# Rows of the second x chunk behind the first load, shorter dummy run, full-array last products and a new order in an attention and gated-MLP kernel

## Chip, cores and metric

The kernel runs on one core of a Trainium2 chip. Its metric is the device time of one execution in microseconds (us), as a median over runs. The core has five engines that work side by side, each with its own queue of instructions: TensorE (PE: matmuls, with weight loads shown apart as PEld), VectorE (DVE), ScalarE (ACT), GpSimd (POOL) and SyncE (SP, which here only issues transfers).

## The reference

The two blocks read the same x and are mixed by a gate for each row. S = 2048 rows, D = 512, 32 heads of 16 columns, F = 1376; inputs and output are bf16.

```python
q, k, v = split_heads(x @ wqkv)                       # 32 heads, 16 columns each
p = softmax(einsum("bhqd,bhkd->bhqk", q, k) * 16 ** -0.5)
a = merge_heads(einsum("bhqk,bhkd->bhqd", p, v)) @ wo
b = ((x @ w_gate) * (x @ w_up)) @ w_down
g = sigmoid((x * gate_w).sum(-1, keepdims=True))
out = g * a + (1 - g) * b
```

## The kernel before

**Tiling.** Four chunks of 512 query rows, four blocks of eight heads in each, and each block in two halves of four heads make 32 groups. A group has 16 steps, one for each tile of 128 keys. A step has four cells: a cell is a 128x512 tile of scores in one of the eight PSUM banks (`ps`). Nearly all matmuls use a 64x32 piece of the PE array (`pe64`, lines 1720 to 1730; `held`, line 1704, is the same product on weights that are still in the array). Four such products side by side make one job, and the two halves `r` of the array's rows work as two queues.

**Two ways through the exponential.** A step of kind "A" is exponentiated by ScalarE (`exp`, line 1816), which takes one cell (128x512) or two at once if their banks are neighbours (128x1024). A step of kind "D" goes to VectorE (`dpass`, line 1854), which makes an approximate exponential by integer arithmetic; three shifted copies of it are made by GpSimd or VectorE (`copy`, line 1866), and PE multiplies all four with scaled copies of V (`pv`, line 1748; `Vs`). So a D step costs 24 more matmuls than an A step and no ScalarE time.

**Order of the work.** Nothing loops on the chip. A planner (`_Sched`) runs when the program is built: it keeps a clock of its own, has costs for every job, and at each moment lets each engine take the next job. Its choices are governed by some 40 tables in `PAR`, each a list of runs (count, value), one entry for each microsecond of the planner's clock, read by `g()`. `apair` lets a new pair of score jobs take two banks together (0: no; 1 and 2: two neighbours; 3 and 4: any two if no neighbours are free; with 2 and 4 the job waits when there are none). `dl` is the most D steps in a group; `alook`, `amax`, `dlook` and the like are limits on what is under way. Other scalars tell the planner when things of the head are there: `t0` the first scores, `tx` the chunks of x, `tw` the weights, `sp0` SP's queue. Each engine then executes its list in that order, with semaphore waits.

**The head** (`prologue`, line 2049) is written out by hand. SP and ScalarE's queue each issue two loads of the first 512 rows of x (into a `DB` buffer), then the first 128 columns of wk (SP) and wq (ScalarE's queue). SP goes on with the rows of chunk 1 into `OT` (two loads of 256 KB), eight transposing loads for chunks 2 and 3, the rest of wk and wq, and later the loads into `QM`. GpSimd's queue loads wv and the gate's weights once wk and wq are there. PE runs six dummy products on constants (`dummy`), transposes the first rows, runs five more dummies (`dummy2`, line 2143), and computes the first Q and K (line 2139), from which the first scores follow. Chunk 1 is transposed on PE (`x_turn`, line 1804).

**The tail.** After the last group, `tail_norm` (line 1971) normalises the output of the last half block in two halves of 256 rows, into `OT[:, 3]`. `tail_out` (line 1982) then adds the last product with wo (`wq[:, 1]` holds its rows) to four banks, one for each tile of 128 output rows, scales by the gate, adds the MLP part (`part_`) and stores. Each tile gets its product in two jobs of half the array's rows, which follow one another. Tiles 0 and 2 are finished by one fused VectorE operation; tiles 1 and 3 are scaled by ScalarE into `oc` and `oraw`, and added by GpSimd (tile 1) and VectorE (tile 3).

## Time and profile before

| | |
|---|---|
| median of 3 runs | 660.68 us (659.93 to 662.45) |
| profiled execution | 659.11 us, its span 657.3 us |
| PE busy | 650.2 us (99%), 22739 matmuls |
| ScalarE busy | 640.3 us (97%) |
| VectorE busy | 606.6 us (92%) |
| GpSimd busy | 523.1 us (80%) |
| first scores start | 8.82 us |
| normalisation of the last half block starts | 649.45 us |

The span runs from the first to the last instruction. A row of the profile gives an engine, a line of the kernel, the operation, what it writes and reads with shapes, and a count; behind the bar stand busy time, mean ns of one, and the idle time before with what ended it. PE's busy time counts any matmul under way, and matmuls overlap, so a busy PE may still have room. In rows in order of time the first column is the start, the second the duration.

### The profile page before, as it was taken

How to read it: one execution, taken by the hardware profiler on the slowest of the kernel's cores; microseconds unless marked ns; L12 is line 12 of the kernel's file. 1: busy time of each engine (PE TensorE's matmuls, PEld its weight loads, DVE VectorE, ACT ScalarE, POOL GpSimd, SP SyncE). 2: the span in 40 equal slices, each digit the busy share in tenths (PEclk: the TensorE clock that was granted, in tenths of full speed). 3: DMA queues.
4: the chain of work that ended last, by engine and by line, in shares of the span. 5: the costliest groups of instructions: out<-in, count | busy, mean ns of one | idle time of the engine just before them, and what ended most of it. 6: DMA issues, size and time to landing. Idle time of an engine off the chain costs nothing.

```text
span 657.3 us, 46640 instructions
## 1 busy us (share of the span) xinstructions
PE 650.2 (99%) x22739; PEld 364.1 (55%) x20515; DVE 606.6 (92%) x1002; ACT 640.3 (97%) x812; POOL 523.1 (80%) x607
## 2 busy tenths in 40 slices
PE   8999999999999999999999999999999999999997
PEld 4565555555555654555555655555555665555653
DVE  6999999999998899999999899999999789989895
ACT  5999999999999999999999999999999999999995
POOL 2537898898987978899998889989898859556772
PEclk9999999999999999999999999999999999999999
DMA  9101212221210110101011010100101010000101
GB/s 181 62 4 45 64 42 72 33 57 48 69 46 20 25 34 19 30 6 34 9 23 29 22 44 12 30 13 14 29 6 41 15 47 20 15 22 19 32 9 46
DMA packets 32114, 22.89 MB, mean 35 GB/s; under 512 B 17356, under 2 KB 28524, under 8 KB 31920
## 3 DMA queue, kind: packets, MB, share of 16 engines
q1 hardware_dynamic: 30784, 18.86, 11.5%
q8 instruction: 169, 2.77, 1.7%
q0 software_dynamic: 176, 0.53, 0.3%
q10 hardware_dynamic: 960, 0.52, 0.3%
q14 instruction: 25, 0.20, 0.1%
HBM read 12.23 MB, written 2.36 MB: 22 GB/s over the span
## 4 chain that ended last, share of the span: by engine, by line
PE 98%; DMA 1%; DVE 0%; issue 0%; ACT 0%; ACTq 0%
PE ps L1727 87%; PE ps L1705 10%; DMA wq<-in_A_wqkv_dram 1%; PE ps L2139 0%; DVE hT L2009 0%; DVE hT L2006 0%; ACT wu L1824 0%; ACTq L2056 0%; PE ps L1811 0%; ACTq L82 0%
## 5 line engine op out<-in xcount | busy, mean ns | idle before, releaser
L1727 PE MATMUL ps<-QM,KT 64*32 64x512 bf16 x5968 | 450.4, 378 | 0.3 <-ACT wu L1824 0.3
L1864 DVE TENSOR_SCALAR DB<-ps 128x512 int16<-128x512 f32 x563 | 367.8, 687 | 27.0 <-PE ps L1727 24.0
L1871 POOL INT64_ADD DB<-DB x374 | 330.8, 900 | 75.6 <-DVE DB L1864 19.2
L1824 ACT ACTIVATE PT<-ps 128x1024 bf16<-128x1024 f32 (+1 forms) x368 | 313.5, 950 | 0.5 <-PE ps L1705 0.3
L1727 PE MATMUL ps<-DB,Vs 64*17 64x512 bf16 x3424 | 300.6, 376 | 0.1
L1824 ACT ACTIVATE xT<-ps 128x1024 bf16<-128x1024 f32 (+1 forms) x271 | 240.8, 965 | 0.2
L1727 PEld LDWEIGHTS ps<-QM,KT 64*32 64x32 bf16 x5968 | 135.4, 89 | 146.2 <-DVE DB L1864 34.8
L1705 PE MATMUL ps<-QM,KT 64*32 64x512 bf16 x2224 | 215.9, 376 | 0.0
L1727 PE MATMUL ps<-PT,Vp 64*17 64x512 bf16 x1274 | 176.7, 376 | 0.0
L1727 PE MATMUL ps<-xT,Vp 64*17 64x512 bf16 x974 | 144.8, 376 | 0.0
L1727 PE MATMUL ps<-DB,Vp 64*17 64x512 bf16 x1128 | 109.5, 377 | 0.0
L1727 PE MATMUL ps<-xT,wg 64*32 64x512 bf16 x1376 | 105.8, 376 | 0.0
L1727 PE MATMUL ps<-xT,wu 64*32 64x512 bf16 x1376 | 105.0, 377 | 0.0
L1727 PEld LDWEIGHTS ps<-DB,Vs 64*17 64x17 bf16 x3424 | 81.6, 86 | 30.1 <-PE ps L1727 7.7
L1727 PE MATMUL ps<-wd,hT 64*32 64x512 bf16 x1408 | 97.4, 376 | 0.0
L1824 ACT ACTIVATE wd<-ps 128x1024 bf16<-128x1024 f32 (+1 forms) x83 | 67.8, 936 | 0.0
L1871 POOL INT64_ADD DB<-wv x65 | 52.8, 828 | 6.4 <-DVE wv L1864 2.6
L1864 DVE TENSOR_SCALAR wv<-ps 128x512 int16<-128x512 f32 (+1 forms) x70 | 47.3, 701 | 2.9 <-PE ps L1727 2.1
L1727 PEld LDWEIGHTS ps<-PT,Vp 64*17 64x17 bf16 x1274 | 43.8, 86 | 10.7 <-PE ps L1727 1.4
L1871 POOL INT64_ADD DB<-wk x49 | 39.9, 830 | 12.2 <-DVE wk L1864 9.3
L1871 POOL INT64_ADD wv<-DB x47 | 44.1, 940 | 6.9 <-DVE DB L1864 4.0
L1871 POOL INT64_ADD wk<-DB x46 | 41.7, 910 | 8.4 <-PE ps L1727 2.3
(120 smaller groups left out, 879.4 us busy)
## 6 DMA issues: line engine op xcount, KB each, us to landing
rb<-rscr SPq DMA_DIRECT2D x16, 256.0 KB
QM<-qraw SPq DMA_DIRECT2D x124, 16.0 KB, 2.2
oc<-oraw SPq DMA_DIRECT2D x60, 32.0 KB, 2.3
out_dram<-ost SPq DMA_DIRECT2D x12, 128.0 KB, 1.7
wd<-in_B_w_down_dram SPq DMA_DIRECT2D x10, 128.0 KB, 2.0
wu<-in_B_w_up_dram SPq DMA_DIRECT2D x12, 96.0 KB, 2.0
wg<-in_B_w_gate_dram SPq DMA_DIRECT2D x12, 96.0 KB, 1.9
OT<-in_A_x_dram SPq DMA_DIRECT2D x2, 256.0 KB, 5.1
```

The lines of the kernel that those rows point to most:

```text
L1705: return pe.add_instruction(mybir.InstMatmult(name=self.nc.get_next_instruction_name(), engine=pe.engine, ins=[pe.lower_ap(rhs), pe.lower_ ...
L1727: o = pe.matmul(dst, lhs, rhs, start=st, stop=sp, tile_position=(64 * r, 32 * cc), skip_group_check=True)
L1824: return self.P.op("act", lambda a: a.activation(dst, src, ACT.Exp, scale=self.ES), deps)
L1864: return self.dve(lambda v: v.tensor_scalar(dst, src, self.YB, 0.0, ALU.add, ALU.max), deps)
L1871: return self.P.op("pool", lambda e: e.int64_add(o.bitcast(I64), a.bitcast(I64), 32 * v * 0x0001000100010001), deps)
```

## The change

1. **Rows held back.** The first of the two loads of chunk 1's rows waits until the first load of x has landed (`d_x[0]`). SP's queue is in order, so all behind it follows.
2. **Fewer dummies.** `dummy2` issues three products instead of five.
3. **Last products on the full array.** In `tail_out` each tile's last product is one 128x128 matmul instead of two jobs of four 64x32 ones; it waits for its half of the normalisation and for the bank's earlier products.
4. **Fourth tile on VectorE.** Tile 3 is finished by the fused VectorE operation from PSUM, as tiles 0 and 2 are; tile 1 stays with ScalarE and GpSimd.
5. **Order anew.** All tables of `PAR` are replaced, now mostly in runs of 2 entries instead of 3, with 648 entries instead of 652. `t0` goes from 9.2 to 8.15, `sp0` from 16.0 to 16.6, and `tx` and `tw` change. The planner's allowance for the tail goes from 4.5 to 3.8 us. The set of key tiles that may be D steps (`dks`) and the sizes of all buffers stay.

```diff
@@ _Sched.tail2
-        self.end = t + 4.5
+        self.end = t + 3.8
@@ _Hw.tail_out
-        for h in (0, 1):
-            for tt, r in ((2 * h, 0), (2 * h + 1, 1), (2 * h + 1, 0), (2 * h, 1)):
-                lo, hi = 64 * r, 64 * r + 64
-                mms = [
-                    (self.ps[32 * cc : 32 * cc + 32, banks[tt], :], self.OT[lo:hi, 3, 128 * tt + 32 * cc : 128 * tt + 32 * cc + 32], self.wq[lo:hi, 1, :], False, True, cc)
-                    for cc in range(4)
-                ]
-                dn[tt] = self.pe64(r, mms, [mul[h], dn[tt] or fa[tt]])
-        ac = {}
-        for tt in (1, 3):
-            tmp = (self.oc if tt == 1 else self.oraw)[:]
-            ac[tt] = P.op("act", ... activation(tmp, self.ps[:, b, :], ACT.Copy, scale=g), [dn[tt]] + deps)
+        for tt in range(4):
+            def full(pe, tt=tt):
+                return pe.matmul(
+                    self.ps[:, banks[tt], :], self.OT[:, 3, 128 * tt : 128 * tt + 128], self.wq[:, 1, :], start=False, stop=True, skip_group_check=True
+                )
+            dn[tt] = P.op("pe", full, [mul[tt // 2], fa[tt]], "pex")
+        ac = P.op("act", lambda a: a.activation(self.oc[:], self.ps[:, banks[1], :], ACT.Copy, scale=self.gq[:, 13:14]), [dn[1]] + deps)
-        for tt in (0, 1, 2, 3):
+        for tt in range(4):
...
-            if tt % 2:
-                c = P.op("pool" if tt == 1 else "dve", ... tensor_tensor(self.hT[:, tt, :], tmp, self.part_[:, tt, :], ALU.add), [ac[tt]] + deps)
+            if tt == 1:
+                c = P.op("pool", lambda v: v.tensor_tensor(self.hT[:, 1, :], self.oc[:], self.part_[:, 1, :], ALU.add), [ac] + deps)
             else:
                 c = self.dve(... scalar_tensor_tensor(self.hT[:, tt, :], self.ps[:, b, :], g, self.part_[:, tt, :], ALU.mult, ALU.add), [dn[tt]] + deps)
@@ _Hw.prologue
-                    o = ld("sp", dst, src, "dxt%d" % ch)
+                    o = ld("sp", dst, src, "dxt%d" % ch, [d_x[0]] if t == 0 else [])
...
-            for i in range(5):
+            for i in range(3):
                 o = pe.matmul(self.ps[:, 4 + i % 4, :], one[:, 0:128], one, start=True, stop=True)
@@ PAR
- 'apair': ((41, 0), (6, 1), (3, 0), (3, 1), (27, 0), (9, 1), (3, 0), (15, 2), ...
+ 'apair': ((2, 0), (4, 1), (3, 0), (3, 2), (8, 0), (2, 1), (6, 0), (2, 4), (20, 3), (18, 0), ...
...
- 'sp0': 16.0,
+ 'sp0': 16.6,
- 't0': 9.2,
- 'tw': [(('wk', False), 0), (('wq', False), 0), (('wk', True), 18.8), (('wq', True), 20.6), (('wv',), 12.6), (('gw',), 16.0)],
- 'tx': [6.5, 8.0, 12.6, 17.0],
+ 't0': 8.15,
+ 'tw': [(('wk', False), 0), (('wq', False), 0), (('wk', True), 20.0), (('wq', True), 21.2), (('wv',), 12.0), (('gw',), 14.0)],
+ 'tx': [5.9, 8.0, 13.6, 18.8],
```

## The prediction

> **What bounds the kernel now.** I read the page first (shares of the engines, chain), then the busy times by stretches, then ScalarE's instructions by shape in two stretches, and last the two ends of the span in order of time.

> ```profile
> span 657.3 us, 46640 instructions
> PE 650.2 (99%) x22739; PEld 364.1 (55%) x20515; DVE 606.6 (92%) x1002; ACT 640.3 (97%) x812; POOL 523.1 (80%) x607
> ...
> PE 98%; DMA 1%; DVE 0%; issue 0%; ACT 0%; ACTq 0%
> ```

> A busy share of 99% says little for PE, whose matmuls overlap; the count of matmuls in equal stretches says more. The columns are PE, weight load, VectorE, ScalarE, GpSimd, each with its instructions.

> ```profile
> core 0: us, PE busy (x) PEld busy (x) DVE busy (x) ACT busy (x) POOL busy (x), PEclk, DMA share, GB/s
> 20.00:40.00 20.00, 19.68 (x709) 11.45 (x631) 18.25 (x38) 18.94 (x34) 5.07 (x8) 1.00 0.04 12
> 150.00:200.00 50.00, 50.00 (x1740) 28.05 (x1560) 46.37 (x76) 50.00 (x56) 44.10 (x50) 1.00 0.19 54
> 300.00:350.00 50.00, 50.00 (x1772) 26.41 (x1636) 48.92 (x81) 49.96 (x84) 48.00 (x50) 1.00 0.10 26
> 400.00:450.00 50.00, 50.00 (x1793) 28.07 (x1612) 48.28 (x79) 50.00 (x56) 45.30 (x53) 1.00 0.07 18
> 550.00:600.00 50.00, 50.00 (x1828) 28.13 (x1600) 46.41 (x75) 49.83 (x58) 32.26 (x42) 1.00 0.07 17
> ```

> PE does 1740 to 1828 matmuls in 50 us, so it has up to 5% of room; ScalarE is busy 49.8 to 50.0 of 50 in all of them, whatever PE does. In the body ScalarE is the engine without slack, and what it gets done depends on how its work is cut. Its exponentials by shape, first in 300 to 350 us, then in 400 to 450 us:

> ```profile
> L1824 ACT ACTIVATE PT<-ps 128x512 bf16<-128x512 f32 x47 | 26.4, 704 | 0.0
> L1824 ACT ACTIVATE PT<-ps 128x1024 bf16<-128x1024 f32 x15 | 15.8, 1071 | 0.0
> L1824 ACT ACTIVATE xT<-ps 128x512 bf16<-128x512 f32 x14 | 9.5, 728 | 0.0
> L1824 ACT ACTIVATE xT<-ps 128x1024 bf16<-128x1024 f32 x8 | 8.6, 1076 | 0.0
> ```

> ```profile
> L1824 ACT ACTIVATE xT<-ps 128x1024 bf16<-128x1024 f32 x34 | 33.0, 1039 | 0.0
> L1824 ACT ACTIVATE PT<-ps 128x1024 bf16<-128x1024 f32 x22 | 22.0, 1039 | 0.0
> ```

> A cell is one 128x512 tile of scores. The first stretch does 61 single cells and 23 pairs, 107 cells; the second 56 pairs, 112 cells. Same 50 us, 5 cells more where all are pairs.

> **The head: rows held back, fewer dummies.** The start, from the chain and in order of time:

> ```profile
> 1.67 5.16 DMA wq<-in_A_wqkv_dram
> 6.96 1.93 PE ps L2139 x24
> ```

> ```profile
> 0.77 2.72 PE L2115 MATMUL ps<-const-bfloat16-1.0 128*128 128x512 bf16 x6 [0.77 <-PEq L2460]
> ...
> 2.13 1.02 SPq L2056 DMA_DIRECT2D OT<-in_A_x_dram  x2
> ...
> 3.19 10.35 SPq L2056 DMA_TRANSPOSE xT<-in_A_x_dram  x8
> ...
> 4.97 1.25 PE L2146 MATMUL ps<-const-bfloat16-1.0 128*128 128x512 bf16 x5
> 5.17 0.60 ACT L2133 ACTIVATE xT<-ps 128x512 bf16<-128x512 f32 x1 [0.20 <-PE ps L2124]
> ...
> 8.82 0.41 PE L1727 MATMUL ps<-QM,KT 64*32 64x512 bf16 x8
> ...
> 9.16 0.23 PEld L1811 LDWEIGHTS ps<-ident,OT 128*128 128x128 bf16 x4 [0.23 <-issue]
> ```

> ```profile
> 1.50:5.00 3.50, 3.50 (x22) 2.16 (x21) 2.53 (x15) 2.08 (x3) 1.92 (x3) 1.00 0.75 208
> 5.00:5.50 0.50, 0.50 (x5) 0.26 (x4) 0.50 (x1) 0.33 (x1) 0.45 (x1) 1.00 1.13 330
> 5.50:6.00 0.50, 0.50 (x4) 0.11 (x2) 0.00 (x0) 0.27 (x1) 0.00 (x0) 1.00 1.12 367
> 6.00:6.50 0.50, 0.23 (x2) 0.00 (x0) 0.00 (x0) 0.00 (x0) 0.00 (x0) 1.00 1.28 343
> ```

> ```profile
> OT<-in_A_x_dram SPq DMA_DIRECT2D x2, 256.0 KB, 5.1
> ...
> DB<-in_A_x_dram SPq DMA_DIRECT2D x2, 128.0 KB, 2.6
> ...
> wq<-in_A_wqkv_dram ACTq DMA_DIRECT2D x1, 128.0 KB, 5.2
> ```

> PE waits for the first columns of wq, landed at 6.83; everything of the head hangs on that. The four loads of x, wq and wk are six of 128 KB, 786 kB. From 1.5 to 5.0 us 208 GB/s x 3.5 us = 728 kB went. Were all of it theirs, 58 kB would be left, 0.2 us at 330 GB/s; instead the two loads into OT (512 KB) share the queues from there on, and wq ends 1.6 us later. Held behind the first x load (landed about 0.73 + 2.6 = 3.3 us), the OT loads issue about 1.2 us later and their bytes come after wq's. wq's bytes then end near 5.3, landing (0.3 to 0.9 us after the last bytes) 5.6 to 6.2; I take 5.95, 0.9 us earlier. The cover that remains: ScalarE's fourth copy of xT ends at 5.17 + 0.60 = 5.77, and three dummies of 0.25 us end at 4.97 + 0.75 = 5.72, where five end at 6.22 and would now cost 0.2 us. So removing two dummies is worth nothing alone, and needed for the rest. The ends are 0 (the OT rows were not what held wq up) and 6.96 - 5.85 = 1.1. **Head: -0.9 us.**

> What queues behind the waiting OT loads on SP's queue: eight transposes (10.35 us of issue), the rest of wk and wq, the first four QM loads, all some 1.2 us later. The x1 rows, 5.1 us from issue to landing before, need about 4 with wq out of the way, so 7.5 to 8.2 against their first use at 9.16 - 0.9 = 8.26: just in time. Chunks 2 and 3 of xT are first needed by K products behind the first eight key tiles, which ScalarE reaches only about half way through the first group (some 20 us a group: 640 us for 32). That hides 1.2 us; without it the whole 1.2 us could come back, which is inside the end 0. ScalarE's load queue and GpSimd's are not passed; GpSimd's wv load waits for wq and wk and goes earlier with them.

> [...] The rows: six dummies take 2.72 us, 0.45 each, the later five 0.25 each, and the granted clock reads 1.00 even where PE is busy 0.23 of 0.5. [...] By the rows the faster rate was reached before 4.97, and the gap after three dummies, 5.72 to about 6.05, is shorter than the 6.22 to 6.96 of now.

> **The tail: full-array products, fourth tile on VectorE.**

> ```profile
> 651.30 0.11 PEld L1727 LDWEIGHTS ps<-wq,OT 64*32 64x32 bf16 x8 [0.47 <-DVE OT L1980]
> 651.58 0.42 DVE L1980 TENSOR_TENSOR OT<-ps,rb 128x256 bf16<-128x256 f32 x1 [0.33 <-ACT rb L1979]
> 651.83 0.34 PEld L1727 LDWEIGHTS ps<-wq,OT 64*32 64x32 bf16 x16 [0.42 <-PE ps L1727]
> 652.28 0.69 ACT L1998 ACTIVATE oc<-ps,gq 128x512 f32<-128x512 f32 x1 [0.73 <-PE ps L1727]
> 652.34 1.50 DVE L2009 SCALAR_TENSOR_TENSOR hT<-ps,gq,wu 128x512 bf16<-128x512 f32 x2 [0.34 <-PE ps L1727]
> ...
> 653.15 1.26 POOL L2006 TENSOR_TENSOR hT<-oc,wu 128x512 bf16<-128x512 f32 x1 [10.18 <-DVE hT L2009]
> 653.76 1.20 DVE L2006 TENSOR_TENSOR hT<-oraw,wu 128x512 bf16<-128x512 f32 x1
> ```

> Now each tile needs two half-array jobs in series (0.42 us waits between them), so VectorE, free at 652.00, starts at 652.34, does two fused products (0.75 each) and a plain add (1.20), and ends at 654.96. With one full product a tile (0.25 as the dummies go, about 0.5 with weights and latency, from 651.3) tile 0 is ready near 651.85, before VectorE is; tiles 2 and 3 near 652.5 and 652.75. VectorE then runs 652.03 + 3 x 0.75 = 654.28, 0.68 earlier; the three stores on SP's queue follow their tiles. Late next is tile 1: ScalarE 652.03 + 0.69, GpSimd + 1.26 + 0.05 = 654.03, which stays ahead. Ends: 0.3 (the start alone) and 0.75. **Tail: -0.65 us.**

> The row for a change of tile shape is the transpose product at 9.16 in the midst of 64*32 jobs: 0.23 us of idle before its weights. On tile 0 that makes 652.08 instead of 651.85, 0.05 late at most. [...]

> **The order anew.** The diff gives no order, only the planner's tables, so I bound the term by ScalarE's rows. The table "apair", which lets a score job take two neighbouring banks, is zero for all 50 entries of 300 to 350 us (107 cells) and nonzero for 38 of 400 to 450 (112): 5/38 = 0.13 cell per entry. Over 20 to 650 us the new table has 55 more nonzero entries (18 of them in 20 to 50, 20 in 300 to 350, 8 fewer in 350 to 400): 55 x 0.13 = 7.2 cells of 50/112 = 0.446 us, 3.2 us of ScalarE. Of the 18 before 50 us I count half, since ScalarE was idle 1.06 us in 20 to 40 and other work limits there: 46 entries, 2.7 us. PE must follow with 0.4% more matmuls a stretch, well inside 1740 to 1828. The other tables move too, and their sign is open. The stretches shown lie 88 matmuls of 1786 apart; a quarter of that as a stretch's spread, 1.2%, makes 0.4% over ten independent ones, 2.6 us either way; a bigger gain, 6 us, is 1% and would still leave PE under its best stretch. **Order: -2.7 us**, ends +2.6 and -6. VectorE and GpSimd (92%, 80%) hide what pairs cost them.

> **The sum.** 0.9 + 0.65 + 2.7 = 4.25. The profiled execution took 659.11 (span 657.3 and 1.8 around it), 1.57 below the median of the runs, 660.68: 654.9 for such an execution, **656.4** for the median. About 0.5%, 3.3 us, is what a measurement of this kernel can tell from no change.

> **Rivals.**
> - The order is neutral: pairs wait longer for neighbouring banks than they save. For it: PE matmuls do not rise with pairs (1740 in a stretch of 56 exponentials). Only the ends gain, 660.68 - 1.55 = 659.1.
> - The order gains more, 6 us, as if the stretches came near the 1828 of the best: 653.1.
> [...]
> - Slower: ScalarE starves at 20 to 50 us. There 24 entries instead of 6 ask for pairs, and early on K, V and Q products hold banks too; where no neighbours are free ScalarE idles. It was idle 1.06 of 20. From 4.9 us more idle (a sixth of these 30 us) it eats the ends' 1.55 and 3.3 beyond: 664 or more. Against it: 22 of the 24 hold a value that falls back to one bank or to two that are not neighbours; only two refuse.

> **How the numbers follow.** Forecast 0.46 (own range 655 to 658), neutral order 0.25, larger order 0.14, head lost 0.09, slower 0.06. The range takes in the larger and the neutral order: 653.2 to 660.2. Faster by over 3.3 us (below 657.4): 0.36 of the forecast's, 0.14, and 0.07 of the next two: 0.57; slower 0.06; between 0.37.

> **What would show it.** Head: first projection near 6.05, first scores near 7.95, OT landed by 8.3. Tail: the third fused product ends 2.3 us after the normalisation, not 2.96. Order: well under 61 singles in 300 to 350 us, and fewer between 20 and 50. It is wrong if ScalarE shows idle time at 20 to 50, if x1's transposes wait for their rows, or if singles fall and PE's count a stretch does not rise.

## The result, and the profile after

The changed kernel took 655.90 us (median of 4 runs, 655.56 to 656.15); the kernel before, beside it, 661.27 us (4 runs, 659.93 to 662.45). The ratio is 0.9919, with a 95% interval of 0.9898 to 0.994: 5.4 us less. Its profiled execution took 656.15 us, against 659.11 before. The experiments below repeat the comparison twice, on two chips, and the ratio was 0.9961 both times (0.9943 to 0.998, and 0.9936 to 0.9986), that is 2.6 us. So the changed kernel was faster in all three comparisons, but the first shows the gain about twice as large as the others. Where that difference lies is the main thing the runs showed.

The page of the changed kernel, its first lines and its chain:

```profile
span 654.4 us, 46429 instructions
PE 647.2 (99%) x22685; PEld 363.6 (56%) x20405; DVE 603.9 (92%) x997; ACT 639.8 (98%) x775; POOL 522.1 (80%) x595
...
PE 94%; ACT 4%; POOL 1%; DVE 0%; issue 0%; POOLq 0%; ACTq 0%
```

ScalarE is as busy as before with 37 instructions fewer, and it now has a place of its own in the chain (4%). The stretches that the prediction showed, in the changed kernel:

```profile
core 0: us, PE busy (x) PEld busy (x) DVE busy (x) ACT busy (x) POOL busy (x), PEclk, DMA share, GB/s
20.00:40.00 20.00, 20.00 (x741) 11.86 (x637) 16.94 (x36) 20.00 (x30) 9.12 (x11) 1.00 0.06 15
300.00:350.00 50.00, 50.00 (x1764) 28.02 (x1636) 48.73 (x78) 49.71 (x69) 46.76 (x48) 1.00 0.09 24
400.00:450.00 50.00, 50.00 (x1800) 27.32 (x1607) 48.27 (x79) 49.81 (x56) 47.91 (x56) 1.00 0.07 19
```

And ScalarE's exponentials by shape from 300 to 350 us:

```profile
L1824 ACT ACTIVATE PT<-ps 128x1024 bf16<-128x1024 f32 x23 | 23.1, 1057 | 0.1
L1824 ACT ACTIVATE xT<-ps 128x1024 bf16<-128x1024 f32 x14 | 14.2, 1046 | 0.1
L1824 ACT ACTIVATE PT<-ps 128x512 bf16<-128x512 f32 x26 | 14.1, 657 | 0.1
L1824 ACT ACTIVATE xT<-ps 128x512 bf16<-128x512 f32 x6 | 3.8, 664 | 0.0
```

From 20 to 40 us the gain is plain: PE does 741 matmuls instead of 709, and ScalarE's idle time there is gone (which part of the change did that is taken up at the end). From 300 to 350 us the single cells fell from 61 to 32 as the new tables ask, but the cells did not rise (106, before 107), nor did PE's matmuls (1764, before 1772). ScalarE is now the one with 0.3 us of idle time. Fewer singles gave no more work where PE did not follow. It is much the same over the whole span: counted by shape, ScalarE did 244 singles and 554 pairs before, 168 singles and 594 pairs after, that is 1352 and 1356 cells, and its busy time fell by 0.5 us (640.3 to 639.8).

The head, from the chain and from the issues of transfers, and the tail in order of time:

```profile
3.49 1.75 PE ps L2118 x16
5.24 1.04 PE ps L2140 x3
6.29 1.77 PE ps L2133 x24
```

```profile
OT<-in_A_x_dram SPq DMA_DIRECT2D x2, 256.0 KB, 3.6
...
wq<-in_A_wqkv_dram ACTq DMA_DIRECT2D x1, 128.0 KB, 3.9
```

```profile
649.01 0.60 PE L1989 MATMUL ps<-wq,OT 128*128 128x512 bf16 x2 [1.11 <-DVE OT L1980]
649.29 0.42 DVE L1980 TENSOR_TENSOR OT<-ps,rb 128x256 bf16<-128x256 f32 x1 [0.33 <-ACT rb L1979]
649.63 2.06 DVE L2001 SCALAR_TENSOR_TENSOR hT<-ps,gq,wu 128x512 bf16<-128x512 f32 x3
...
649.86 0.59 PE L1989 MATMUL ps<-wq,OT 128*128 128x512 bf16 x2 [0.24 <-DVE OT L1980]
...
650.53 1.26 POOL L1998 TENSOR_TENSOR hT<-oc,wu 128x512 bf16<-128x512 f32 x1 [8.94 <-DVE hT L2001]
651.82 0.36 ACTq L2007 DMA_DIRECT2D out_dram<-hT  x1
```

The first columns of wq take 3.9 us instead of 5.2, and now the three dummy products end last, not the transfer; the first scores start at 7.98 us instead of 8.82. The normalisation ends at 649.71 (649.29 + 0.42), and the span ends 4.64 us behind it; in the kernel before it was 5.26 us.

### The profile page after: what moved, and what is told of

It reads as the page before. It is cut to its first block, busy times and chain, and to the rows that moved or that the text cites. A ratio compares the mean times of both kernels' runs of the same rounds, so it can differ in the third digit from the quotient of the medians.

```text
span 654.4 us, 46429 instructions
## 1 busy us (share of the span) xinstructions
PE 647.2 (99%) x22685; PEld 363.6 (56%) x20405; DVE 603.9 (92%) x997; ACT 639.8 (98%) x775; POOL 522.1 (80%) x595
## 3 DMA queue, kind: packets, MB, share of 16 engines
q8 instruction: 168, 2.75, 1.7%
## 4 chain that ended last, share of the span: by engine, by line
PE 94%; ACT 4%; POOL 1%; DVE 0%; issue 0%; POOLq 0%; ACTq 0%
PE ps L1727 83%; PE ps L1705 10%; ACT wu L1824 1%; ACT hT L1824 1%; POOL DB L1871 1%; ACT wd L1824 1%; PE ps L2109 0%; ACT wo L1824 0%; PE ps L2133 0%; PE ps L2118 0%; POOLq L87 0%; PE ps L2140 0%; POOL wk L1871 0%; POOL wq L1964 0%; ACT wg L1824 0%
## 5 line engine op out<-in xcount | busy, mean ns | idle before, releaser
L1727 PE MATMUL ps<-QM,KT 64*32 64x512 bf16 x5912 | 444.9, 378 | 0.8 <-ACT wu L1824 0.6
L1871 POOL INT64_ADD DB<-DB x382 | 337.5, 901 | 76.9 <-DVE DB L1864 19.9
L1864 DVE TENSOR_SCALAR DB<-ps 128x512 int16<-128x512 f32 x551 | 359.8, 686 | 22.9 <-PE ps L1727 19.7
L1824 ACT ACTIVATE PT<-ps 128x1024 bf16<-128x1024 f32 (+1 forms) x344 | 303.4, 969 | 1.0 <-PE ps L1727 0.3
L1727 PE MATMUL ps<-DB,Vs 64*17 64x512 bf16 x3440 | 300.0, 376 | 0.3
L1824 ACT ACTIVATE xT<-ps 128x1024 bf16<-128x1024 f32 (+1 forms) x267 | 243.8, 989 | 0.6 <-PE ps L1727 0.3
L1727 PEld LDWEIGHTS ps<-QM,KT 64*32 64x32 bf16 x5912 | 134.0, 89 | 144.7 <-DVE DB L1864 28.7
L1727 PE MATMUL ps<-PT,Vp 64*17 64x512 bf16 x1240 | 170.0, 376 | 0.0
L1727 PE MATMUL ps<-xT,Vp 64*17 64x512 bf16 x996 | 144.3, 376 | 0.0
L1727 PE MATMUL ps<-DB,Vp 64*17 64x512 bf16 x1104 | 106.8, 377 | 0.0
L1727 PE MATMUL ps<-xT,wg 64*32 64x512 bf16 x1376 | 105.6, 377 | 0.0
L1727 PE MATMUL ps<-xT,wu 64*32 64x512 bf16 x1376 | 105.5, 376 | 0.0
L1727 PE MATMUL ps<-wd,hT 64*32 64x512 bf16 x1408 | 100.9, 376 | 0.0
L1727 PEld LDWEIGHTS ps<-DB,Vs 64*17 64x17 bf16 x3440 | 82.9, 86 | 30.4 <-PE ps L1727 5.7
L1824 ACT ACTIVATE wd<-ps 128x1024 bf16<-128x1024 f32 (+1 forms) x83 | 69.4, 941 | 0.0
L1871 POOL INT64_ADD DB<-wv x53 | 47.6, 915 | 13.7 <-PE ps L1727 6.2
L1864 DVE TENSOR_SCALAR wv<-ps 128x512 int16<-128x512 f32 x72 | 47.9, 685 | 3.9 <-PE ps L1727 3.3
L1727 PEld LDWEIGHTS ps<-PT,Vp 64*17 64x17 bf16 x1240 | 42.5, 86 | 9.8 <-PE ps L1727 2.0
L1864 DVE TENSOR_SCALAR wk<-ps 128x512 int16<-128x512 f32 x68 | 44.9, 687 | 2.8 <-PE ps L1727 2.4
L1727 PEld LDWEIGHTS ps<-wd,hT 64*32 64x32 bf16 x1408 | 36.2, 92 | 12.1 <-issue 0.8
## 6 DMA issues: line engine op xcount, KB each, us to landing
rb<-rscr SPq DMA_DIRECT2D x16, 256.0 KB
out_dram<-ost SPq DMA_DIRECT2D x12, 128.0 KB, 1.7
wd<-in_B_w_down_dram SPq DMA_DIRECT2D x10, 128.0 KB, 2.2
OT<-in_A_x_dram SPq DMA_DIRECT2D x2, 256.0 KB, 3.6
```

What stands on the lines that cost most here:

```text
L1727: o = pe.matmul(dst, lhs, rhs, start=st, stop=sp, tile_position=(64 * r, 32 * cc), skip_group_check=True)
L1824: return self.P.op("act", lambda a: a.activation(dst, src, ACT.Exp, scale=self.ES), deps)
L1864: return self.dve(lambda v: v.tensor_scalar(dst, src, self.YB, 0.0, ALU.add, ALU.max), deps)
L1871: return self.P.op("pool", lambda e: e.int64_add(o.bitcast(I64), a.bitcast(I64), 32 * v * 0x0001000100010001), deps)
```

## The experiments

All are compared with the kernel before on the same chip. The last column sums the rows in which PE's weight loads wait and the profile shows no cause but "issue" (explained under the first experiments). 2.4 to 4.2 us of each sum are rows of this kind in the head and the tail, where the cause is another, as said there.

| run | kernel | median us (runs) | ratio, 95% interval | profiled us | waits for "issue", us |
|---|---|---|---|---|---|
| before | | 660.68 (3) | | 659.11 | 10.1 |
| after | whole change | 655.90 (4) | 0.9919, 0.9898 to 0.994 | 656.15 | 11.3 |
| e0 | before, unchanged | 661.38 (12) | 0.9984, 0.9963 to 1.0004 | 660.59 | 11.3 |
| e1 | head alone | 661.28 (12) | 0.9983, 0.9959 to 1.0008 | 663.83 | 18.0 |
| e2 | tail alone | 661.27 (12) | 0.9973, 0.995 to 0.9995 | 661.21 | 12.4 |
| e3 | order alone | 661.93 (12) | 0.9977, 0.9957 to 0.9997 | 662.98 | 17.1 |
| e4 | whole change | 661.10 (8) | 0.9961, 0.9943 to 0.998 | 661.23 | 18.2 |
| e5 | all but the tail | 660.80 (6) | 0.9954, 0.9936 to 0.9972 | 660.99 | 17.3 |
| e6 | all but the head | 661.35 (5) | 0.996, 0.9945 to 0.9975 | 661.24 | 14.7 |
| e7 | whole, six dummies | 660.22 (11) | 0.9946, 0.9924 to 0.9967 | 662.53 | 18.9 |
| e8 | before, unchanged | 664.21 (12) | 0.9988, 0.9965 to 1.001 | 661.71 | 14.3 |
| e9 | whole change | 662.35 (12) | 0.9961, 0.9936 to 0.9986 | 663.83 | 19.0 |
| e10 | whole, more transfers | 674.41 (6) | 1.0158, 1.0112 to 1.0205 | 674.40 | 29.8 |
| e11 | whole, one dummy | 661.87 (12) | 0.9954, 0.9934 to 0.9975 | 660.83 | 17.0 |

e0 to e3 ran on one chip, e4 to e7 on a second, e8 to e11 on a third; the kernel before, run beside them, had medians of 662.53, 663.72 and 664.54 us there. The chip of the first two rows is not known. e0 and e8 are the kernel before itself, so their 0.9984 and 0.9988 show how far a ratio can lie from 1 with no change at all.

**The parts one by one (e0 to e3).** My theory was the sum of the prediction: the parts add up. The edits are those of the change's own diff, one part at a time; e0 is the kernel before once more, as a measure of the comparison itself. Its profiled span was 658.8 us, 1.5 us longer than in the first execution of the same kernel, so that one was on the short side.

> The kernel before, unchanged, to see how far its own runs and its profiled execution lie apart: its median was 661.27 us while its profiled execution took 659.11. If that execution was an ordinary one, its span comes out at 657 to 658 again and the runs at 660 to 662; if it was a lucky one, the span comes out some 2 us longer, and the trace of before understates what the new order saves.

> Old order and old tail; only the held-back rows and three dummies instead of five. My theory (the head shifts everything behind it): 0.85 us less than before, the first scores at 7.98 us instead of 8.82, about 660.4 us. Rival (the old order was laid out for scores at 9.2 on its clock and rows of chunks 2 and 3 at 12.6 and 17.0; the later transposes and the earlier start make waits that eat the gain): same as before, 661.3 us, with PE or ScalarE waits between 13 and 40 us that before did not have.

```diff
-                    o = ld("sp", dst, src, "dxt%d" % ch)
+                    o = ld("sp", dst, src, "dxt%d" % ch, [d_x[0]] if t == 0 else [])
...
-            for i in range(5):
+            for i in range(3):
```

> Old order and old head; only the new tail. My theory: 0.6 us less than before, 660.7 us, and 7.24 us from the start of the last normalisation to the end instead of 7.85. Rival (the change of tile shape costs as much as it saves): 661.3 us, 7.85.

e2 has `tail_out` of the changed kernel, and everything else of the kernel before (the planner's allowance too, 4.5).

> The new tables with the old head and the old tail. My theory, that the parts add up: the whole change took 5.4 us off the median, head and tail take 1.45 of it, so 3.9 us less than before, 657.4 us; by the two traces alone the order gives 1.45 us, 659.8 us. Rival (the new order was fitted to the earlier start and stalls behind the old head): as before or slower, 661 us or more.

e3 has the changed kernel's `PAR` and its allowance for the tail (3.8), and all else of the kernel before. e5 has that allowance too. It only enters the planner's estimate of the end.

Against e0, the same program as before, the ratios moved by 0.0001, 0.0011 and 0.0007: at most 0.7 us each, less than the intervals are wide. Together they make 1.3 us, not the 5.4 of the first measurement. No part came out at its forecast: the medians of e1 and e2 lie 0.1 us under that of e0, and e3's 0.55 us above it, which is what its rival had foretold (661 us or more). From this I formed a second theory: the order was laid out for the new head, and in a kernel where the two do not fit, transfers and PE's fetches of instructions fall on each other. For it spoke the row of waits that the profile puts down to nothing it shows. In the changed kernel the weight loads' rows of that kind are

```profile
PEld ps L1727 <- issue: 7.7, 28, 0.6
PEld ps L2109 <- issue: 1.8, 5, 0.7
PEld ps L1989 <- issue: 0.7, 1, 0.7
PEld ps L1811 <- issue: 0.5, 2, 0.2
PEld ps L2140 <- issue: 0.3, 1, 0.3
PEld ps L2133 <- issue: 0.3, 1, 0.3
```

(total, how often, longest; 11.3 us in all), while in e1 and e3 the first of these rows stood at 15.1 and 13.8 us. Only that first row, nearly all of it between the head and the tail, can be read as waiting for instructions. The others have known neighbours: the row of the dummies begins with the span's first 0.74 us, the weights of the last products wait for the normalisation, and in the kernel before the weights of the first projections show 1.2 us of "issue" while the product behind them waits for the transfer of wq:

```profile
6.93 0.46 PEld L2139 LDWEIGHTS ps<-xT,wq 128*128 128x128 bf16 x8 [1.20 <-issue]
6.96 0.61 PE L2139 MATMUL ps<-xT,wq 128*128 128x128 bf16 x8 [0.74 <-DMA wq<-in_A_wqkv_dram]
```

The first row alone is 6.3 us in the kernel before; in e0 to e11 it is 7.2, 15.1, 8.5, 13.8, 14.7, 14.9, 10.5, 14.9, 10.9, 15.9, 26.1 and 13.9.

**The whole change again, and without one part (e4 to e7).**

> The changed kernel once more, beside the parts, on their chip. If its 655.9 belongs to the kernel, it is again 655 to 657 with the kernel before at 660 to 662, a ratio near 0.992, its runs close together, and issue waits of TensorE near 7.7 us in the profile. If it belonged to the chip or to the hour, it gives 658 to 661, as each part alone did, a ratio near 0.997, and scatters over 5 us as they do.

> New order and new head, old tail. Theory (head and order were made for each other, the tail is apart): 0.6 more than the changed kernel, near 656.5, with issue waits of 7 to 9 us and the last normalisation at about 647 us. Rival (the tail takes part in the interlock, or the gain was the chip's): 660 to 661.

> New order and new tail, old head (rows of the second chunk not held back, five dummy products). Theory (the order fits only the new head): the order's gain goes, 660 to 661.5, of which the head itself explains 0.9, and TensorE waits 12 to 15 us for its instructions. Rival (the parts add up): 656.8, that is the changed kernel's time and the 0.9 of the head, with issue waits of 7 to 9 us.

> The changed kernel with six dummy products in place of three: the rows are still held back and the first projection weights still land at 5.6 us, but the projections start about 0.75 us later (three products at 0.25 us on the full clock). Theory (the order was laid out for the times of the new head, and a start 0.75 us later brings the transfers and TensorE's instruction fetches against each other): 659 to 662 and issue waits of 11 to 15 us. Rival 1 (only the delay counts): 656.7, issue waits as before. Rival 2 (the order needs the second chunk's rows and the first weights in their new sequence, not the start of the scores): near 656 to 656.7, without new waits.

```diff
-            for i in range(3):
+            for i in range(6):
```

The second theory fell. The kernel whose parts do fit, e4, had 661.1 us and 18.2 us of waits, as many as the misfits (e5 17.3 and e7 18.9, where 7 to 9 and 11 to 15 had been expected); without the head (e6) or without the tail (e5) it was no slower than their share, 0.25 us slower and 0.3 us faster. e7 started its first scores 0.9 us later than e4 (9.12 against 8.20) and lost nothing that can be measured. The 655.9 us, then, were not the kernel's alone: e4 is the same program, instruction for instruction, and its profiled execution took 5.1 us longer.

Two executions of one program show where the time goes. ScalarE's instructions in e4 fall behind those of the first execution in small steps, 0.2 to 0.6 us each, spread over the whole span and now and then partly made good (1.3 us behind at 60 us of the span, 2.3 at 185, 3.6 at 260, 2.6 at 410, 4.2 at 585, 5.0 at the end). One such step, first in the first execution of the changed kernel, then at the same instructions of e4, weight loads in order of time:

```profile
164.60 0.10 PEld L1727 LDWEIGHTS ps<-DB,Vs 64*17 64x17 bf16 x4
164.70 0.10 PEld L1727 LDWEIGHTS ps<-xT,wg 64*32 64x32 bf16 x4
```

```profile
165.99 0.17 PEld L1727 LDWEIGHTS ps<-DB,Vs 64*17 64x17 bf16 x4
167.12 0.10 PEld L1727 LDWEIGHTS ps<-xT,wg 64*32 64x32 bf16 x4 [0.95 <-issue]
```

The very same job stands 0.95 us in the one and not at all in the other, with no engine or transfer that it waits for. The row that collects such waits is, against the 7.7 us above,

```profile
PEld ps L1727 <- issue: 14.7, 49, 1.0
```

The windows around the step, again the first execution and then e4:

```profile
150.00:250.00 100.00, 100.00 (x3560) 55.34 (x3212) 94.55 (x152) 99.93 (x114) 86.52 (x96) 1.00 0.15 41
```

```profile
150.00:250.00 100.00, 99.31 (x3481) 54.98 (x3145) 92.69 (x148) 98.73 (x110) 84.68 (x94) 1.00 0.15 41
```

The transfers are the same (41 GB/s) and so is the clock; PE did 79 matmuls fewer in e4, and ScalarE was idle 1.3 us. What PE waits for I read from q8, a queue of kind "instruction". First the changed kernel, then e4 and e9, which are the same program:

```profile
q8 instruction: 168, 2.75, 1.7%
```

```profile
q8 instruction: 168, 2.75, 1.8%
```

```profile
q8 instruction: 168, 2.75, 1.9%
```

2.75 MB in 168 packets are 16 KB each, for PE's 43,090 recorded instructions: one packet for about 256 instructions, or every 3.9 us. I take each for a fetch of PE's next instructions. The share of 16 engines' time makes 0.017 x 16 x 654.4 / 168 = 1.06 us for a fetch in the first execution, 1.13 in e4, 1.20 in e9. Between the head and the tail the weight loads of the fourteen traces have 246 standstills of over 0.3 us put down to "issue", and 218 of them end 1.1 to 1.6 us after such a packet has landed (18 of 21 in e4; but 5 of 9 in the first execution of the changed kernel); of all weight loads, 13% start in that stretch. They also come at steps of a block: of PE's recorded instructions the one at 167.12 us is number 10,401, and others that stood in e4 are 15,000 (18 x 256 further, less 9), 38,531 and 39,042 (2 x 256 further, less 1). I read this so: PE reaches the end of what it has before the next block is usable, in some executions more often than in others. Most blocks cost nothing here, since the row L1727 counts 22 to 49 waits for 168 blocks; but these waits add up to 6.3 to 15.9 us in an execution of this kernel.

**The same chip, more transfers, one dummy (e8 to e11).** The third theory: the parts add up, each is small, and on top of them lie the instruction waits of the chip and the moment. From the two profiles of the changed kernel, a us of waits costs 5.08 / 6.9 = 0.74 us.

> The kernel before, treated as the next one is, on the same chip, for the size of the change. Theory (instruction fetches): its profiled execution has 9 to 12 us in which TensorE's weight loads wait for instructions, and lies at 651.6 us and 0.74 us for each us of these waits (the slope is that between the two profiles of the changed kernel: 656.15 with 11.3 us, 661.23 with 18.2 us). Rival (the chips differ in something else, such as the clock or the engines' speed): the waits are as ever and the time lies 2 us or more off that line.

> The changed kernel beside the kernel before. Theory (the parts add up, about 0.5 us for the head, 0.5 for the tail and 1 for the order, and more or fewer instruction waits lie on top): 1.5 to 4 us under the kernel before, ratio 0.994 to 0.998; the profiled execution at 647.8 us and 0.74 us for each us of the weight loads' waits for instructions. Rival (the first measurement was the kernel's own): 5 us under it, ratio 0.992, waits near 11 us again.

> The changed kernel, with 250 additional copies of 128 KB within the device's memory, one behind every third exponential on ScalarE, on SP's queue; their target is read by nobody. Theory (TensorE's waits are late instruction fetches, and the core's own transfers slow these): the mean of a 16 KB fetch rises from 1.1 to 1.25 us or more, the weight loads' waits for instructions from 11 to 18 us to over 22, and the time by 4 to 12 us. Rival (what slows the fetches is outside the core: fetches with no transfer beside them took 1.02 to 1.12 us, others 1.06 to 1.15, hardly more): waits and time within 1.5 us of the changed kernel's.

```diff
+        h = self.exs = getattr(self, "exs", []) + [o]
+        n = len(h) // 3
+        if len(h) % 3 == 0 and n <= 250:
+            self.P.dma("sp", lambda e: e.dma_start(self.big[128 * n - 128 : 128 * n, :], self.x2[0:128, :]), [h[-3]], "dex")
```

> The changed kernel with one dummy product in place of three. Reading of the head (the dummies took 0.42 us each and ended last, the weights were there at 5.6 us): the projections start at 5.7 us instead of 6.3, and the first scores at 7.3 to 7.6 us instead of 8.0, if the full clock comes at 5.9 us all the same. Rival (the dummies bring the full clock, and an idle stretch in their place puts it off): 24 projections at half clock take 3 us or more instead of 1.77, first scores at 8.4 us or later. In the whole time both are under what the runs can tell, within 1 us of the changed kernel.

```diff
-            for i in range(3):
+            for i in range(1):
```

The size of the change held at 0.9961 (e9), or 1.9 us between e9 and e8. The line from waits to time held in part: e8 had more waits than the 9 to 12 us expected, and should have had 651.6 + 0.74 x 14.3 = 662.2 us and had 661.71; e11 660.4, and had 660.83; e9 661.9, and had 663.83, a miss of 1.9. A straight line through twelve profiled executions (all but e7 and e10, with a term for each part) gives 0.84 us for each us of waits, with a standard error of 0.09, and leaves 0.7 us of scatter; its terms for the parts (head -2.0, tail +0.3, order -2.0, each with 0.5 of error) differ by about 1 us from what the traces show directly at the two ends, 0.89 and 0.63 us less. It has no term for the chip.

e10 bears the theory out in its size and not in its detail (its line 1728 is line 1727 of the others).

```profile
big<-in_A_x_dram SPq DMA_DIRECT2D x250, 128.0 KB, 2.7
```

```profile
PEld ps L1728 <- issue: 26.1, 66, 0.9
...
PE ps L1728 <- issue: 2.5, 9, 0.5
```

```profile
q8 instruction: 168, 2.75, 1.8%
```

The waits rose from 19.0 to 29.8 us and the time by 12.1 us against e9, and 40 of the 41 standstills of over 0.3 us end 1.1 to 1.6 us after a fetch has landed. So the core's own transfers do cost instruction waits: at 0.74 to 0.84 they make 8 to 9 of the 12 us. The rest is at least partly direct: the loads into `rb` (DMA rb<-rscr) came into the chain with 1.1% of the span, 7 us, though part of that may be time the instruction waits would otherwise have taken. But a fetch itself did not get longer (0.018 x 16 x 672.6 / 168 = 1.15 us, e9 1.20); I had expected 1.25 or more. So it is not the packet's own time that the other transfers stretch. Nor does a block become usable later: the standstills end 1.41 us after the landing in the median, in e9 1.44. What is left is that the fetch starts later, and the packets do start a little later against PE's own instructions, by 12 of them in the median against e9, about 0.2 us. Why they do stays open.

e11 started its projections when wq landed, and they ran at full speed:

```profile
5.10 0.63 PE L2140 MATMUL ps<-const-bfloat16-1.0 128*128 128x512 bf16 x1
5.96 0.61 PE L2133 MATMUL ps<-xT,wq 128*128 128x128 bf16 x8 [0.23 <-DMA wq<-in_A_wqkv_dram]
```

First scores came at 7.82 us. That is later than the 7.3 to 7.6 expected, since wq landed later than in the first execution, and earlier than the 8.4 of the rival with half the clock. It does not show that the idle stretch is harmless at any time: the full clock came at 5.79 us, just before the projections. In the median e11 stands beside e9 (661.87 against 662.35), with no difference that can be told. No kernel here is measurably better than the changed one.

## Why the prediction came out as it did

**The time.** 656.4 was forecast and 655.9 came. The closeness is luck as far as the whole goes: the two ends came out as worked out, but the largest term, the order, did not work as foretold, and the first execution had fewer waits than the later ones. The forecast gain was 4.25 us; the first comparison gave 5.4, the two others 2.6 and 2.2 (663.72 - 661.10 and 664.54 - 662.35). By those two the change is within the 0.5% that the prediction gave as the bound of what can be told.

**Head, -0.9: right in its own stretch; what it is worth in the whole is not shown.** The first scores stand at 7.98, 7.93, 8.20, 7.45 and 7.66 us in the executions with the new head and three dummies (after, e1, e4, e5, e9) and at 8.82, 8.79, 8.73, 8.63, 8.98 and 8.43 in the six with the old one: 7.84 against 8.73 on average, 0.89 less. The cause is as foretold: the rows of chunk 1 no longer share the queues with wq, which takes 3.9 us instead of 5.2. Two details were off, and they cancelled. wq landed at 1.67 + 3.9 = 5.57, not 5.95; and the three dummies, which were to end at 5.72, took 0.35 to 0.42 us each, where 0.25 had been assumed, ended at 6.28 and so set the start. That the first projection started at 6.12, near the 6.05 foretold, is in part luck. And the earlier start is not yet time off the whole. In the medians the head was worth 0.1 us (e1 against e0) and 0.25 us (e4 against e6), each with some 2 us of uncertainty, and e7 lost its 0.9 us at the start without a loss in the whole. The forecast took it that the lead is kept to the end; no run here shows that.

**The dummies and the clock.** The dummies ran slow where the full clock came later: in the executions shown below, 0.27 us each where it came before them (e9, at 4.43 us), and 0.46 where it came only during the last of them (e4, at 6.26). The trace's own record of the granted clock has the step to its full share, 1.0, at 4.94 us in the kernel before and at 5.91 in the changed one, and in the others anywhere from 3.62 to 6.75 us; in these two, behind a step down near the end, it has the share 0.5. The time from the first step to the step down is 651.946 us in the kernel before and 645.119 in the changed one, and in the others one of these two, 655.359 or (e10) 662.186 us. In order of size these differ by 6.827, 3.413 and 6.827 us, and they are 189, 191, 192 and 194 times 3.4133 us (645.119 / 189). So in these records the two steps lie a whole number of 3.413 us apart; the first step itself lies anywhere within a stretch of 3.13 us although all these programs begin alike. What sets it is not shown. The column PEclk, on which the prediction relied, cannot show the step: it reads 1.00 from 1.5 to 5.0 us too, where the dummies took 0.45 us each. The projections started after the step in all executions but e10, where the step came 0.12 us into them, at 6.57, and they took 1.99 us instead of 1.93. So no run shows the projections at the slow rate of the first dummies (0.45 us each against 0.25) for longer than those 0.12 us. What the time of the step does cost is the dummies' time, as two executions with equal heads show, e9 and e4:

```profile
4.93 0.81 PE L2140 MATMUL ps<-const-bfloat16-1.0 128*128 128x512 bf16 x3
5.80 0.61 PE L2133 MATMUL ps<-xT,wq 128*128 128x128 bf16 x8
```

```profile
5.13 1.38 PE L2140 MATMUL ps<-const-bfloat16-1.0 128*128 128x512 bf16 x3
6.34 0.61 PE L2133 MATMUL ps<-xT,wq 128*128 128x128 bf16 x8
```

0.54 us between the starts of the projections, more than half of the head's gain.

**Tail, -0.65: right.** From the start of the last shuffle to the end of the span it was 7.47 or 7.48 us in all six kernels with the old tail, and 6.83 to 6.85 in all eight with the new: 0.63 less, the steadiest number of the study. Nothing comes behind this stretch that could lose it again, though medians cannot show so little (e2 lies 0.1 us under e0, and e5, with the old tail, 0.3 us under e4). VectorE's third fused product ended 649.63 + 2.06 - 649.71 = 1.98 us after the normalisation, even earlier than the 2.3 foretold (before 2.96). What then came late was tile 1, by ScalarE and GpSimd, at 651.79, as named. The 0.23 us of idle taken over from the row at 9.16, for a change of tile shape, do not come again between products of one shape: the two full products of a pair took 0.60 us together (649.01 to 649.61), with nothing between them.

**Order, -2.7: the mechanism fell, the size is not settled.** Pairs rose and singles fell, as the table asked (61 to 32 in 300 to 350 us). But the step "0.13 cell for each entry of the table" was wrong: for the 20 new entries there it gives 2.6 cells more, and the cells did not rise at all (107 to 106), nor did PE's matmuls (1772 to 1764), as the rival of a neutral order had argued. That singles fall and PE's count does not rise is one of the signs by which the prediction said it would be wrong. Its other signs did not come: ScalarE did not lose time at 20 to 50 us. ScalarE was read as the engine without slack and PE as one with up to 5% of room. In fact each us that PE stands for instructions goes with 0.74 to 0.84 us of time, so PE has little reserve; that its matmul counts differ by stretch with the kind of work is likely, but not shown. Nor can the order claim the gain from 20 to 40 us, of which I had counted half. There e1, with the old order and the new head, and then e3, with the new order alone, show

```profile
20.00:40.00 20.00, 20.00 (x730) 11.73 (x648) 18.65 (x39) 19.64 (x33) 4.45 (x6) 1.00 0.05 13
20.00:40.00 20.00, 18.75 (x665) 10.95 (x587) 16.47 (x35) 18.38 (x29) 7.14 (x10) 1.00 0.05 12
```

ScalarE is idle 0.36 us with the head alone and 1.62 us with the order alone, against 0.82 to 1.30 in the four executions with neither; e6, with order and tail, has 0.49. So the idle time goes with the new head at least as much as with the order. Between the ends of the profiled executions the body from the first scores to the last normalisation took 649.45 - 8.82 = 640.63 us before and 647.16 - 7.98 = 639.18 after, 1.45 less, with 1.2 us more waits; but this holds the stretch from 20 to 40 us, and so a part of the head's gain. By the ratios, with order against without (e3 and e0, e6 and e2, e5 and e1), it is 0.0007, 0.0013 and 0.0029, on average 0.0016 or 1.1 us, give or take about 1.2, and the last two of these compare runs of different chips. The line through twelve executions gives 2.0 at equal waits. That is 1 to 2 us, less than 2.7, which none of the three quite excludes.

**Why the first measurement showed 5.4.** 0.89 + 0.63 + 1 to 2 make 2.5 to 3.5 us, if the head's lead counts in full: what the two later comparisons show and a little more. The remainder goes with the waits: 11.3 us in the first execution of the changed kernel, 17 to 19 in its others, while the kernel before had 10.1, 11.3 and 14.3. Its four runs lay within 0.6 us of each other, those of e9 within 8.3 (658.05 to 666.37). That instruction waits make most of the difference between the first execution and e4 is shown, by the standstills at the ends of blocks; why the first had so few of them is not, and e9 lies 1.9 us off the line. On each chip the executions with the new head had more waits than those with the old one (11.3 against 10.1; 18.0 against 11.3 to 17.1; 17.3 to 18.9 against 14.7; 17.0 and 19.0 against 14.3), although the waits for wq, which the sum counts too, got shorter. So the head may lose all of its 0.9 us again this way; with one profiled execution of each kernel this stays open.

## What to carry to other kernels

When parts of a change are worth less than 1 us each in a program of 650, read each from its own stretch of the trace, and not from medians, which here could not tell 0.6 us with twelve runs. The stretch behind the last normalisation repeated within 0.02 us, the start of the first scores within about 0.4 us either way. A shorter stretch at the end of the span is time gained; an earlier start is so only if what follows keeps its lead, and that has to be read separately. Before putting down a difference of a few us to the change, compare the rows "<- issue" of TensorE's weight loads and the queue of kind "instruction" in both profiles, and run the same program again, at another time and on another chip: here that alone was 5 us. An engine that is 100% busy by its overlapping records may look as if it had room and still have little reserve; the test is what a wait on it costs, here 0.74 to 0.84 us for each us that TensorE stood.
